# Mask by quadrants, a product on three tiles at once, and a recomputed order in an attention and two-MLP kernel

## The chip, the cores and the metric

One core of a Trainium2 chip runs the whole program. The metric is the device time of one execution in microseconds, a median of several runs. TensorE (PE) multiplies, VectorE (DVE), ScalarE (ACT) and GpSimd (POOL) work on elements, and SyncE (SP) issues every DMA. Each engine has its own list of instructions and works through it in that order.

## The reference

Three layers follow each other, in float32. The matrices of the MLPs come as float64 and are turned into float32 on the chip.

```
scores = q @ k.T / sqrt(64)          # 4 batches, 8 heads, 576 rows, head size 64
keep score (i, j) where 0 <= i - j < 64, else -1e9; softmax; attn @ v
x  = attention as 2304 x 512
h  = x @ w_in                        # first MLP, 512 -> 1024
solu = h * softmax(h); ln = layer norm(solu) * g_ln
x2 = ln @ w_out                      # 1024 -> 512, "the second product of the first MLP"
h  = x2 @ w_in                       # second MLP, 512 -> 2048
g  = (a0 + a1 h + a2 h^2 + a3 h^3) / (1 + |b0||h| + |b1|h^2 + 1e-6)
out = g @ w_out                      # 2048 -> 512
```

## The kernel before

The 2304 rows are 18 tiles of 128. Every product of float32 accuracy is made as three products of halves: the operand is split into a rounded high part and a low rest (`wi`, `xh`/`xl`, `lh`/`ll`), and high x high, low x high and high x low are added up in one PSUM bank.

Two phases follow each other on TensorE.

**Phase one** takes the 18 tiles through attention and the first MLP. A tile t goes through `scores` (tile `s`, lines 295 to 312: the mask is added first, line 304, as a product with an identity matrix of 128 rows, then 16 products of 64 x 64 quarters of the array, line 309), the row maximum on VectorE (`soft_max`), eight exponentials on ScalarE, the sums' reciprocals on VectorE (`soft_sum`, tile `rc`), the scaling on GpSimd (`soft_norm`, line 334), transposes on TensorE (`pt`), copies, `attend` (`pv`), the split (`xh`, `xl`), the first product (`h`, lines 441 to 451, 24 products of 512 columns into one single PSUM tile `h`), the solu and layer norm (`st`, `e`; VectorE and ScalarE in turn), transposes (`pl`), their split (`lh`, `ll`), and for each pair of tiles the second product (`x2_mm`, lines 521 to 530; the trace calls its output `x`). That one has four blocks `dc`, each of 24 products of 256 columns, and its result goes to memory (`x2d`).

The float64 weights are converted by a chain of steps on ScalarE and VectorE for each piece of 128 x 512 (`cv_step`, lines 391 to 418; `cv_hi`, `cv_lo`): eight pieces `wi` of the first MLP's first matrix, eight pieces `wo` of its second one, and 32 pieces `cc` of the second MLP, which are spilled to memory (`w2d`). All eight `wi` are needed for the first `h`, all eight `wo` for the first block of `x2`.

**Phase two** runs the second MLP in six blocks of three tiles (`g_mm` with output `hp`, `o_mm` with output `o`). Its weights are loaded back from `w2d` and split (`w2_hi`, `w2_lo`, tile `w`), its inputs from `x2d` (`x_hi`, `x_lo`, tiles `x2h`, `x2l`).

The order of all this is not written out. Each step is added to a planner (class `Schedule`, lines 31 to 158) with its engines, a duration, the steps it needs, the buffers it takes and gives back (the rings in `RINGS`) and, for some, a wanted time from the tables `WANT` and `PACE`. `latest` works out a due time for each step, `arrange` picks, engine by engine, the step that is due first of those that could start, and the instructions are emitted in that order. A step with two engines, as `"DVE|POOL"`, goes to the second where the planner thinks that it is free sooner.

Of the kernel before, what the change touches and what calls it, by code (L numbers as in the profile page):

```python
# [28 lines left out]
class Schedule:  # L29
# [15 lines left out]
    def add(self, key, engine, dur, want, needs, fn, *args, take=(), give=()):  # L45
        assert key not in self.steps, key
        self.steps[key] = [engine.split("|"), dur if isinstance(dur, tuple) else (dur,), want, list(needs), fn, args,
                           take, give]
        for g in give:
            self.givers.setdefault(g, []).append(key)  # L50

    def latest(self):
# [35 lines left out]
        return due  # L88
# [80 lines left out]
RINGS = {"q": 2, "k": 2, "v": 4, "s": 1, "P": 2, "tr": 2, "PT": 4, "o": 2, "x": 2, "h": 1, "e": 2, "lnT": 3, "xs": 1,  # L169
# [5 lines left out]
def attention_moe_moe2(ctx: ExitStack, tc, q, k, v, w1, w1o, g_ln, w2, w2o, num, den, out):  # L175
# [61 lines left out]
    masks = ap.tile([P, 3, P], BF16, name="masks", tag="masks", bufs=1)  # L237

    def constants():
# [11 lines left out]
        for i in range(3):  # L251
            for b in range(2):
                rows = slice(64 * b, 64 * b + 64)
                nc.gpsimd.tensor_copy(masks[rows, i, :], band[rows, 64 * b:64 * b + P])

        nc.gpsimd.memset(masks[0:64, 1, 0:64], NEG)
        nc.gpsimd.memset(masks[64:128, 2, 0:64], NEG)

    def mask_of(t):
        return masks[:, 1 if t * P % S == 0 else 2 if (t * P + 64) % S == 0 else 0, :]  # L260
# [34 lines left out]
    def scores(t):  # L295
# [7 lines left out]
        for j in range(2):  # L303
            nc.tensor.matmul(s[j], ib, mask_of(t).unsqueeze(1).broadcast_to([P, NPAIR, P]), start=True, stop=False)
# [27 lines left out]
    def soft_norm(t, j, eng):  # L332
        sl = slice(NPAIR * j, NPAIR * j + NPAIR)
        eng.tensor_tensor(out=Pn[t][:, j], in0=Pn[t][:, j],  # L334
                          in1=stat[t][2][:, sl].unsqueeze(2).broadcast_to([P, NPAIR, P]), op=ALU.mult)
# [48 lines left out]
    def w1_load(c):  # L384
# [3 lines left out]
        for hf in range(2):  # L388
            tiles["cv", ("i", c, hf)] = x[:, hf, :]

    def cv_step(key, part, eng=None):
# [28 lines left out]
    def cv_hi(key, scale, eng):  # L420
        hi, lo = hi_lo(key)
        A = tiles["cv", key][4]
        if scale is None:
            copy(eng, hi, A)
        elif eng is nc.scalar:
            eng.activation(hi, A, AF.Copy, scale=scale)
        else:
            eng.tensor_scalar_mul(hi, A, scale)

    def cv_lo(key, scale, eng=None):  # L430
        hi, lo = W[key][:, 0, :], W[key][:, 1, :]
        if scale is None:
            sub(eng, lo, tiles["cv", key][4], hi)
# [98 lines left out]
    def x2_out(pr, dc, eng):  # L532
        if dc == 0:
            tiles["xs", pr] = mp.tile([P, 2, KC, P], F32, name=f"xs{pr}", tag="xs", bufs=1)
        copy(eng, tiles["xs", pr][:, :, dc, :], tiles["x2", pr, dc].rearrange("p (t c) -> p t c", t=2))

    def x2_store(pr):
        nc.sync.dma_start(x2d[:, 2 * pr:2 * pr + 2], tiles["xs", pr])
# [4 lines left out]
    for t in range(NTILE):  # L543
        def step(name, engine, dur, needs, fn, *args, want=None, take=(), give=()):
            needs = [n if isinstance(n, tuple) else (n, t) for n in needs]
            want = None if want is None else H0 + t * T + want
            add((name, t), engine, dur, want, needs, fn, *args, take=take, give=give)

        pr, c0 = divmod(t, 2)
# [8 lines left out]
        step("scores", "PE", 1.45, ["load_q", "load_k", ("constants", 0)], scores, t, want=WANT["scores"],  # L558
             take=[("s", t), ("P", t)], give=[("q", t), ("k", t)])
        for j in range(2):  # L560
            step(f"max{j}", "DVE", 0.8, ["scores"], soft_max, t, j)
            for n in range(4):
                step(f"exp{j}{n}", "ACT", 0.58, [f"max{j}"], soft_exp, t, j, n, give=[("s", t)])
            step(f"sum{j}", "DVE", 0.35, [f"exp{j}{n}" for n in range(4)], soft_sum, t, j)
            step(f"norm{j}", "POOL|DVE", (1.15, 0.6), [f"sum{j}"], soft_norm, t, j)
        for j in range(2):
            step(f"probs{j}", "PE", 0.45, [f"norm{j}"], probs_T, t, j, want=WANT[f"probs{j}"], take=[("tr", (t, j))],
                 give=[("P", t)])
            step(f"probs_copy{j}", "ACT|DVE", (0.58, 0.62), [f"probs{j}"], probs_copy, t, j, take=[("PT", (t, j))],
# [3 lines left out]
        step("att_hi", "ACT|DVE", (0.58, 0.62), ["attend"], attended_hi, t)  # L573
        step("att_lo", "DVE", 0.62, ["att_hi"], attended_lo, t, give=[("o", (t, 0))])
# [4 lines left out]
        step("solu_max", "DVE", 1.2, ["h3"], solu_max, t, take=[("e", t)])  # L579
        step("solu_exp", "ACT", 1.3, ["solu_max"], solu_exp, t)  # L580
# [329 lines left out]
```

## Time and profile before

| | us |
|---|---|
| median of 3 runs | 739.9 (738.57 to 739.94) |
| the profiled execution, own time | 739.92 |
| its span, first to last instruction | 738.1 |
| TensorE busy | 699.2 |
| VectorE busy | 615.2 |
| ScalarE busy | 487.6 |
| GpSimd busy | 64.9 |

The profile lists each instruction with its start, its duration and, where its engine stood idle before it, what ended the wait. Products on TensorE overlap, so that the price of one is the distance from its start to the next start, not its own duration. The span is 1.8 us shorter than the execution's time.

### The profile page before, as it was taken

How to read it: one execution, taken by the hardware profiler on the slowest of the kernel's cores; microseconds unless marked ns; L12 is line 12 of the kernel's file. 1: busy time of each engine (PE TensorE's matmuls, PEld its weight loads, DVE VectorE, ACT ScalarE, POOL GpSimd, SP SyncE). 2: the span in 40 equal slices, each digit the busy share in tenths (PEclk: the TensorE clock that was granted, in tenths of full speed). 3: DMA queues.
4: the chain of work that ended last, by engine and by line, in shares of the span. 5: the costliest groups of instructions: out<-in, count | busy, mean ns of one | idle time of the engine just before them, and what ended most of it. 6: DMA issues, size and time to landing. Idle time of an engine off the chain costs nothing.

```text
span 738.1 us, 12597 instructions
## 1 busy us (share of the span) xinstructions
PE 699.2 (95%) x4788; PEld 620.6 (84%) x4788; DVE 615.2 (83%) x1016; ACT 487.6 (66%) x970; POOL 64.9 (9%) x65
## 2 busy tenths in 40 slices
PE   1578999999999999999999999999999999999997
PEld 0356788888888888999888999989899889998985
DVE  5999999999999665688999878788877797777874
ACT  5587777777777554586888556665676566666553
POOL 2211111111111111001521000000000000000000
PEclk9999999999999999999999999999999999999999
DMA  8554387878776320345420100100010010001001
GB/s 302 198 188 148 115 266 234 292 240 258 263 235 208 116 86 30 115 143 154 140 71 23 65 0 22 64 2 0 22 65 1 0 52 15 0 1 44 1 0 44
DMA packets 47644, 77.90 MB, mean 106 GB/s; under 512 B 5024, under 2 KB 23456, under 8 KB 47072
## 3 DMA queue, kind: packets, MB, share of 16 engines
q1 hardware_dynamic: 47584, 77.09, 32.1%
q8 instruction: 38, 0.62, 0.4%
q14 instruction: 22, 0.18, 0.1%
HBM read 59.25 MB, written 17.83 MB: 104 GB/s over the span
## 4 chain that ended last, share of the span: by engine, by line
PE 85%; DVE 7%; DMA 3%; ACT 2%; issue 1%; SPq 1%; POOL 0%; DVEq 0%; ACTq 0%; POOLq 0%
PE hp L721 8%; PE hp L720 8%; PE hp L719 8%; PE o L785 8%; PE o L784 8%; PE o L783 8%; PE x L527 5%; PE x L529 5%; PE x L528 5%; PE h L449 4%; PE h L451 4%; PE h L450 4%; PE s L309 3%; PE pv L357 2%; PE pl L509 2%; PE pt L340 2%
## 5 line engine op out<-in xcount | busy, mean ns | idle before, releaser
L721 PE MATMUL hp<-x2h,w 128*128 128x384 f32 x384 | 129.6, 337 | 1.2 <-DVE w L210 1.1
L719 PE MATMUL hp<-x2h,w 128*128 128x384 f32 x384 | 129.3, 337 | 0.0
L720 PE MATMUL hp<-x2l,w 128*128 128x384 f32 x384 | 129.2, 337 | 0.0
L729 ACT ACTIVATE w<-hp,ab 128x768 f32<-128x768 f32 x48 | 43.4, 904 | 115.3 <-PE hp L721 115.1
L785 PE MATMUL o<-w,gl 128*128 128x512 f32 x288 | 113.8, 395 | 0.0
L784 PE MATMUL o<-w,gh 128*128 128x512 f32 x288 | 113.5, 394 | 0.0
L783 PE MATMUL o<-w,gh 128*128 128x512 f32 x288 | 113.2, 393 | 0.0
L737 DVE SCALAR_TENSOR_TENSOR w<-r,b,w 128x768 f32<-128x768 f32 x48 | 49.6, 1033 | 54.9 <-ACT r L731 54.9
L527 PE MATMUL x<-lh,wo 128*128 128x256 f32 x288 | 83.9, 291 | 0.0
L529 PE MATMUL x<-lh,wo 128*128 128x256 f32 x288 | 81.3, 282 | 0.0
L528 PE MATMUL x<-ll,wo 128*128 128x256 f32 x288 | 81.0, 281 | 0.0
L719 PEld LDWEIGHTS hp<-x2h,w 128*128 128x128 f32 x384 | 72.1, 188 | 3.3
L720 PEld LDWEIGHTS hp<-x2l,w 128*128 128x128 f32 x384 | 72.1, 188 | 3.3
L721 PEld LDWEIGHTS hp<-x2h,w 128*128 128x128 f32 x384 | 72.1, 188 | 1.9 <-DVE w L210 1.9
L785 PEld LDWEIGHTS o<-w,gl 128*128 128x128 f32 x288 | 54.0, 188 | 12.6
L449 PE MATMUL h<-wi,xh 128*128 128x512 f32 x144 | 59.2, 411 | 5.1 <-DVE st L466 4.4
L784 PEld LDWEIGHTS o<-w,gh 128*128 128x128 f32 x288 | 54.0, 188 | 9.8
L334 POOL TENSOR_TENSOR P<-P,rc 128x512 f32<-128x512 f32 x36 | 40.5, 1125 | 247.3 <-DVE rc L330 195.0
L783 PEld LDWEIGHTS o<-w,gh 128*128 128x128 f32 x288 | 54.1, 188 | 9.4
L451 PE MATMUL h<-wi,xl 128*128 128x512 f32 x144 | 57.9, 402 | 0.7 <-DVE xl L210 0.7
L450 PE MATMUL h<-wi,xh 128*128 128x512 f32 x144 | 57.5, 399 | 0.0
L323 ACT ACTIVATE P<-s,mx 128x128 f32<-128x128 f32 x144 | 50.7, 371 | 9.7 <-DVE mx L318 7.7
(109 smaller groups left out, 1522.3 us busy)
## 6 DMA issues: line engine op xcount, KB each, us to landing
v<-in_v_dram SPq DMA_DIRECT2D x35, 256.0 KB, 4.4
xc<-in_moe_w_in_dram SPq DMA_DIRECT2D x16, 512.0 KB, 4.3
xc<-in_moe_w_out_dram SPq DMA_DIRECT2D x16, 512.0 KB, 4.1
w2d<-Ac SPq DMA_DIRECT2D x32, 256.0 KB, 3.8
r<-w2d SPq DMA_DIRECT2D x32, 256.0 KB, 3.0
k<-in_k_dram SPq DMA_DIRECT2D x17, 384.0 KB, 4.0
q<-in_q_dram SPq DMA_DIRECT2D x18, 256.0 KB, 5.1
x2d<-xs SPq DMA_DIRECT2D x9, 512.0 KB, 3.9
```

What stands on the lines that cost most here:

```text
L449: nc.tensor.matmul(o, xh[:, c, :], wh, start=(c == 0), stop=False)
L450: nc.tensor.matmul(o, xh[:, c, :], wl, start=False, stop=False)
L451: nc.tensor.matmul(o, xl[:, c, :], wh, start=False, stop=(c == KC - 1))
L527: nc.tensor.matmul(o, wh, lh[:, f, :], start=(f == 0), stop=False)
L528: nc.tensor.matmul(o, wh, ll[:, f, :], start=False, stop=False)
L529: nc.tensor.matmul(o, wl, lh[:, f, :], start=False, stop=(f == FC1 - 1))
L719: nc.tensor.matmul(h, wh[:, sl], xh[:, c], start=(c == 0), stop=False)
L720: nc.tensor.matmul(h, wh[:, sl], xl[:, c], start=False, stop=False)
L721: nc.tensor.matmul(h, wl[:, sl], xh[:, c], start=False, stop=(c == KC - 1))
L783: nc.tensor.matmul(o, gh[:, n, sl], wh, start=(f == 0), stop=False)
L784: nc.tensor.matmul(o, gh[:, n, sl], wl, start=False, stop=False)
L785: nc.tensor.matmul(o, gl[:, n, sl], wh, start=False, stop=(f == FC2 - 1))
```

## The change

- The mask is added by four products of 64 x 64 quarters of the array instead of two of the whole one. Each still streams 512 columns; the mask table has two patterns instead of three and is chosen for each half tile.
- The second product of the first MLP takes three tiles at once: four blocks of 24 products of 384 columns for each three tiles. The tiles `lh` and `ll` grow from 256 to 384 columns and have two buffers instead of three.
- GpSimd keeps the scaling `soft_norm` and the constants; the low parts `w2_lo`, `x_lo` and `cv_lo` stay on VectorE. Steps `cv0` and `cv_hi` of the conversions are ScalarE's alone.
- The first matrix is loaded in eight halves of 512 KB instead of four pieces of 1 MB.
- The planner's durations are replaced, and a new table `SHIFT` of some 560 numbers, one for each kind of step (the first five tiles, the last two, and the rest by class), moves its due time.

```
-            nc.tensor.matmul(s[j], ib, mask_of(t).unsqueeze(1).broadcast_to([P, NPAIR, P]), start=True, stop=False)
+            for b in range(2):
+                rows, cols = slice(64 * j, 64 * j + 64), slice(64 * b, 64 * b + 64)
+                nc.tensor.matmul(s[j][cols], ib[rows, rows], mask_of(t, b)[rows].unsqueeze(1).broadcast_to([64, NPAIR, P]),
+                                 start=True, stop=False)
...
-        o = po.tile([P, 2 * P], F32, name=f"x2_{pr}_{dc}", tag="o")
+        o = po.tile([P, TB], F32, name=f"x2_{pr}_{dc}", tag="o")
...
-        if t % 2 == 1:
+        if c0 == JT - 1:
...
-        x = mp.tile([P, 2, 512], I64, name=f"xi_{c}", tag=("lh", "ll")[c % 2], bufs=3)
-        nc.sync.dma_start(x, w1[c * P:(c + 1) * P, :].rearrange("p (h f) -> p h f", h=2))
+            tiles["w1", c] = mp.tile([P, 2, 512], I64, name=f"xi_{c}", tag=("lh", "ll")[c % 2], bufs=2)
+        x = tiles["w1", c][:, hf, :]
+        nc.sync.dma_start(x, w1[c * P:(c + 1) * P, 512 * hf:512 * hf + 512])
...
-        add(("w2", i), "DVE|POOL", (0.602, 1.225), due + 0.7, [("w2h", i)], w2_lo, f, j, give=[("r2", ("w", i))])
+        add(("w2", i), "DVE", 0.68, due + 0.7, [("w2h", i)], w2_lo, f, j, give=[("r2", ("w", i))])
...
-            add(("x", bk, c), "DVE|POOL", (0.45, 0.956), due + 4.0, [("xh", bk, c)], x_lo, bk, c, give=[("xr", (bk, c))])
+            add(("x", bk, c), "DVE", 0.55, due + 4.0, [("xh", bk, c)], x_lo, bk, c, give=[("xr", (bk, c))])
...
-                due[key] = min([cap.get(key, 1e9)] + ([st[2]] if st[2] is not None else []) +
-                               [due[u] - after for u in users[key]])
+                due[key] = min([cap.get(key, 1e9)] + [due[u] - after for u in users[key]] +
+                               ([st[2] + SHIFT.get(st[8], 0.0)] if st[2] is not None else []))
...
-RINGS = {"q": 2, "k": 2, "v": 4, "s": 1, "P": 2, "tr": 2, "PT": 4, "o": 2, "x": 2, "h": 1, "e": 2, "lnT": 3, "xs": 1,
+SHIFT = {
+    "k_zero.0": 29.34, "v_zero.0": 33.59, "load_q.0": 16.46, "load_k.0": 8.1, "load_v0.0": 62.31, "load_v1.0": 28.99,
...
+RINGS = {"q": 2, "k": 2, "v": 4, "s": 1, "P": 2, "tr": 2, "PT": 4, "o": 2, "x": 2, "h": 1, "e": 2, "lnT": 2, "xs": 1,
```

The instruction lists show where things move. In the names, the first number behind a letter is the tile (`h5`), for `x2` the group of tiles and the block; the last number is a serial one.

TensorE at the start of a tile's scores (`s0_0`, `s0_1`: the two banks). Before, of the first scores in its list:

```order
L304 LDWEIGHTS ib_96
L304 MATMUL s1_0_157<-masks_97,ib_96 128x512
L304 LDWEIGHTS ib_96
L304 MATMUL s1_1_158<-masks_97,ib_96 128x512
L309 MATMUL s1_0_157<-k1_128,q1_130 64x128 x2
L309 MATMUL s1_1_158<-k1_128,q1_130 64x128 x2
```

and in the changed kernel:

```order
L409 LDWEIGHTS ib_96
L409 MATMUL s0_0_179<-masks_97,ib_96 64x512
L409 LDWEIGHTS ib_96
L409 MATMUL s0_0_179<-masks_97,ib_96 64x512
L409 LDWEIGHTS ib_96
L409 MATMUL s0_1_180<-masks_97,ib_96 64x512
L409 LDWEIGHTS ib_96
L409 MATMUL s0_1_180<-masks_97,ib_96 64x512
L415 MATMUL s0_0_179<-k0_140,q0_151 64x128 x2
L415 MATMUL s0_1_180<-k0_140,q0_151 64x128 x2
```

Two weight loads and two products of 128 rows have become four of 64 rows, and all stand ahead of the quarter products as before.

TensorE around the first block of the second product (`x2_0_0`). Before:

```order
L449 MATMUL h3_869<-wi_3_1_430,xh3_833 128x512
L450 MATMUL h3_869<-wi_3_1_430,xh3_833 128x512
L451 MATMUL h3_869<-wi_3_1_430,xl3_834 128x512
L509 MATMUL pl2_0_930<-ident_95,e2_819 128x128 x4
L509 MATMUL pl2_1_939<-ident_95,e2_819 128x128 x4
L527 MATMUL x2_0_0_947<-lh0_648,wo_0_489 128x256
L528 MATMUL x2_0_0_947<-ll0_649,wo_0_489 128x256
L529 MATMUL x2_0_0_947<-lh0_648,wo_0_489 128x256
```

and in the changed kernel:

```order
L415 MATMUL s8_1_1302<-k8_1082,q8_1047 64x128 x2
L415 MATMUL s8_0_1301<-k8_1082,q8_1047 64x128 x2
L415 MATMUL s8_1_1302<-k8_1082,q8_1047 64x128 x2
L415 MATMUL s8_0_1301<-k8_1082,q8_1047 64x128 x2
L415 MATMUL s8_1_1302<-k8_1082,q8_1047 64x128 x2
L629 MATMUL x2_0_0_1338<-lh0_790,wo_0_642 128x384
L630 MATMUL x2_0_0_1338<-ll0_791,wo_0_642 128x384
L631 MATMUL x2_0_0_1338<-lh0_790,wo_0_642 128x384
```

Before, the block stands behind the first product of tile 3 (`h3`) and the transposes of tile 2. In the changed kernel it stands behind `h5` and the scores of tile 8: ahead of it stand scores of 9 tiles, 15 half transposes `pt`, 7 `pv`, 6 `h` and 3 tiles' `pl`, where there were 5, 8, 4, 4 and 3.

VectorE at the last piece `wo`, which that block needs. Before:

```order
L494 TENSOR_SCALAR st2_818<-st2_818 128x1
L435 SCALAR_TENSOR_TENSOR wo_5_880<-Ao_5_766,gT_98,wo_5_880 128x512
L499 TENSOR_SCALAR e2_819<-e2_819,st2_818 128x1024
L435 SCALAR_TENSOR_TENSOR wo_6_892<-Ao_6_779,gT_98,wo_6_892 128x512
L435 SCALAR_TENSOR_TENSOR wo_7_899<-Ao_7_808,gT_98,wo_7_899 128x512
L317 TENSOR_REDUCE mx4_702<-s4_0_705 128x4
L318 TENSOR_SCALAR mx4_702<-mx4_702 128x4
L457 TENSOR_REDUCE st3_944<-h3_869 128x1
```

and in the changed kernel:

```order
L522 ISA Ao_5_820<-co_5_819,ro_5_821 128x1024
L522 ISA Ao_6_1125<-co_6_1124,ro_6_1126 128x1024
L522 ISA Ao_2_1111<-co_2_1110,ro_2_1112 128x1024
L537 SCALAR_TENSOR_TENSOR wo_5_1282<-Ao_5_820,gT_98,wo_5_1282 128x512
L537 SCALAR_TENSOR_TENSOR wo_6_1287<-Ao_6_1125,gT_98,wo_6_1287 128x512
L537 SCALAR_TENSOR_TENSOR wo_2_1295<-Ao_2_1111,gT_98,wo_2_1295 128x512
L423 TENSOR_REDUCE mx8_1298<-s8_0_1301 128x4
L424 TENSOR_SCALAR mx8_1298<-mx8_1298 128x4
```

The last `wo` was row 159 of VectorE's list and is row 203.

SP's queue at the last loads `xo`, from which the last `wo` are made. Before:

```order
L381 DMA xo_4_574<-in_moe_w_out_dram 128x512
L279 DMA k5_581<-in_k_dram 128x4x192
L271 DMA q5_587<-in_q_dram 128x512
L381 DMA xo_5_617<-in_moe_w_out_dram 128x512
L381 DMA xo_6_631<-in_moe_w_out_dram 128x512
L381 DMA xo_7_664<-in_moe_w_out_dram 128x512
L293 DMA v4_0_689<-in_v_dram 128x512
L293 DMA v4_1_727<-in_v_dram 128x512
```

and in the changed kernel:

```order
L396 DMA v4_1_640<-in_v_dram 128x512
L382 DMA k4_720<-in_k_dram 128x4x192
L396 DMA v5_0_769<-in_v_dram 128x512
L396 DMA v5_1_797<-in_v_dram 128x512
L374 DMA q6_877<-in_q_dram 128x512
L374 DMA q7_886<-in_q_dram 128x512
L487 DMA xo_2_933<-in_moe_w_out_dram 128x512
L487 DMA xo_6_967<-in_moe_w_out_dram 128x512
L396 DMA v6_0_1007<-in_v_dram 128x512
```

The last `xo` stood behind `q5` and ahead of the values of tile 4; the last two now stand behind the keys of tile 4, the values of tile 5 and the queries of tiles 6 and 7.

## Rows read from the trace of the kernel before

**Rows 1.** Stretches: length, each engine's busy time (instructions), granted clock, DMA share, GB/s.
```profile
0.00:84.70 84.70, 52.06 (x451) 38.66 (x451) 73.81 (x162) 57.65 (x150) 14.08 (x28) 0.96 0.60 207
84.70:240.00 155.30, 155.28 (x1538) 137.57 (x1536) 150.24 (x359) 115.20 (x329) 22.75 (x20) 1.00 0.73 237
...
320.00:400.00 80.00, 78.77 (x444) 72.93 (x443) 74.89 (x86) 62.37 (x92) 19.75 (x9) 1.00 0.36 104
```
**Rows 2.** Timeline of TensorE at its first second product: start, duration, instruction.
```profile
84.68 0.36 PE L527 MATMUL x<-lh,wo 128*128 128x256 f32 x1
```
**Rows 3.** The chain of waits, one step (`pt`) of two neighbouring tiles: start, duration.
```profile
122.53 0.87 PE pt L340 x8
...
138.36 0.87 PE pt L340 x8
```
**Rows 4.** Timeline of TensorE within one tile of the steady part.
```profile
153.35 0.39 PE L449 MATMUL h<-wi,xh 128*128 128x512 f32 x1
...
154.04 1.03 PE L340 MATMUL pt<-ident,P 128*128 128x128 f32 x8
154.83 0.36 PE L527 MATMUL x<-lh,wo 128*128 128x256 f32 x1
...
157.78 0.61 PE L304 MATMUL s<-masks,ib 128*128 128x512 bf16 x2
158.32 1.10 PE L309 MATMUL s<-k,q 64*64 64x128 f32 x32
159.35 1.15 PE L357 MATMUL pv<-PT,v 128*64 128x64 f32 x32
160.44 0.39 PE L527 MATMUL x<-lh,wo 128*128 128x256 f32 x1
```
**Rows 5.** Timeline of TensorE in phase two: twelve products of 384 columns, then the next.
```profile
481.33 0.33 PE L719 MATMUL hp<-x2h,w 128*128 128x384 f32 x1
...
483.44 0.39 PE L783 MATMUL o<-w,gh 128*128 128x512 f32 x1
```
**Rows 6.** Timeline of VectorE: its first instruction, and the last two pieces `wo`.
```profile
7.42 0.43 DVE L411 TENSOR_SCALAR ci<-ci 128x512 f32<-128x512 f32 x1 [7.42 <-ACT ci L404]
...
82.01 1.41 DVE L435 SCALAR_TENSOR_TENSOR wo<-Ao,gT,wo 128x512 fp32r<-128x512 f32 x2
```
**Rows 7.** VectorE's groups: busy time, mean ns of one | idle before.
```profile
L457 DVE TENSOR_REDUCE st<-h 128x1 f32<-128x1024 f32 x18 | 22.0, 1220 | 11.3 <-PE h L451 11.3
L466 DVE CUSTOM_DVE_ANT_0 e<-h,e 128x1024 f32<-128x1024 f32 x18 | 21.9, 1219 | 5.7 <-ACT e L461 5.7
```
**Rows 8.** Timeline of VectorE: a row maximum up to the next instruction; reciprocals likewise.
```profile
12.13 0.68 DVE L317 TENSOR_REDUCE mx<-s 128x4 f32<-128x512 f32 x1
...
12.93 0.69 DVE L210 TENSOR_TENSOR wi<-Ai,wi 128x512 fp32r<-128x512 f32 x1
...
61.50 0.16 DVE L329 TENSOR_SCALAR rc<-sum 128x4 f32<-128x4 f32 x1
...
61.81 1.22 DVE L466 CUSTOM_DVE_ANT_0 e<-h,e 128x1024 f32<-128x1024 f32 x1
```
**Rows 9.** VectorE's groups that the change takes away ahead of the last `wo`.
```profile
L406 DVE TENSOR_SCALAR co<-xo 128x512 uint32<-128x512 uint32 x2 | 1.7, 835 | 0.0
L216 DVE CAST wi<-Ai 128x512 fp32r<-128x512 f32 x1 | 1.3, 1264 | 0.0
L406 DVE TENSOR_SCALAR ci<-xi 128x512 uint32<-128x512 uint32 x1 | 1.3, 1260 | 0.0
```
**Rows 10.** Timeline of GpSimd and VectorE: a low part on GpSimd, and two equal instructions on VectorE.
```profile
348.12 3.35 POOL L210 TENSOR_TENSOR x2l<-xr,x2h 128x384 fp32r<-128x384 f32 x1 [54.39 <-ACT x2h L702]
...
350.50 1.78 DVE L762 SCALAR_TENSOR_TENSOR t<-t,ab,r 128x768 f32<-128x768 f32 x1
...
370.99 1.01 DVE L762 SCALAR_TENSOR_TENSOR t<-t,ab,r 128x768 f32<-128x768 f32 x1
```
**Rows 11.** DMA issues of the `xo` loads: count, KB each, median us to landing.
```profile
xc<-in_moe_w_out_dram SPq DMA_DIRECT2D x16, 512.0 KB, 4.1
```

More of the change, by code (lines that the diff above doesn't have):

```diff
@@ L87, in latest @@
                         cap[g] = min(cap.get(g, 1e9), d - steps[g][1][0] - self.LATENCY)
-        return due
+        return {k: d + (SHIFT.get(steps[k][8], 0.0) if steps[k][2] is None else 0.0) for k, d in due.items()}
     def arrange(self):
@@ L250, in constants, with mask_of @@
         )
[L251 to L260, printed above, removed]
+        for i in range(2):
+            for j in range(2):
+                rows = slice(64 * j, 64 * j + 64)
+                nc.gpsimd.tensor_copy(masks[rows, i, :], band[rows, 64 * j:64 * j + P])
+        nc.gpsimd.memset(masks[:, 1, 0:64], NEG)
+    def mask_of(t, b):
+        return masks[:, 1 if (t * P + 64 * b) % S == 0 else 0, :]
     raw, values, Pn, stat, PTs, xTs, tiles = {}, {}, {}, {}, {}, {}, {}
@@ L545, in step @@
             needs = [n if isinstance(n, tuple) else (n, t) for n in needs]
-            want = None if want is None else H0 + t * T + want
-            add((name, t), engine, dur, want, needs, fn, *args, take=take, give=give)
-        pr, c0 = divmod(t, 2)
+            if want is not None:
+                want += H0 + t * T
+            cls = str(t) if t < 5 or t > LAST - 2 else f"s{t % JT}" if want is not None else "s"
+            add((name, t), engine, dur, want, needs, fn, *args, take=take, give=give, group=f"{name}.{cls}")
+        pr, c0 = divmod(t, JT)
         if t == 0:
@@ L609, in convert @@
     def convert(key, want, load, last):
+        group = "cv." + "_".join(map(str, key))
         if load is not None:
-            add(("cvl", *key), "DMA", 1.46, None, [], cv_load, key, load, take=[("x64", key)])
-        cvl = ("cvl", *key) if load is not None else ("cvl", *key[:-1])
+            add(("cvl", *key), "DMA", 1.46, None, [], cv_load, key, load, take=[("x64", key)], group=group)
+        cvl = ("cvl", *key)
         give = [("x64", key)] if load is not None else []
-        for part, engine, dur, needs in [(0, "ACT|DVE", (0.67, 0.6), [cvl]), ("r", "ACT", 0.67, ["cv0"]), (1, "DVE", 0.34, ["cv0"]),
-                                         (2, "DVE", 0.34, ["cv1"]), (3, "DVE", 0.62, ["cv2"]), (6, "DVE", 0.62, ["cv3", "cvr"])]:
+        for part, engine, dur, needs in [(0, "ACT", 0.61, [cvl]), ("r", "ACT", 0.61, ["cv0"]), (1, "DVE", 0.42, ["cv0"]),
+                                         (2, "DVE", 0.42, ["cv1"]), (3, "DVE", 0.69, ["cv2"]), (6, "DVE", 0.68, ["cv3", "cvr"])]:
@@ L616, in convert @@
             needs = [(n, *key) if isinstance(n, str) else n for n in needs]
             add((f"cv{part}", *key), engine, dur, None, needs, cv_step, key, part,
[L618 removed]
+                take=[("cA", key)] if part == 0 else [], give=give if part in ("r", 3) else [], group=group)
         needs = [("cv6", *key)]
         if last is cv_spill:
[L621 removed]
+            add(("cv7", *key), "DMA", 0.73, want, needs, cv_spill, key, key[1], give=[("cA", key)], group=group)
@@ L840, in step @@
             needs = [n if isinstance(n, tuple) else (n, p) for n in needs]
-            add((name, p), engine, dur, due, needs, fn, bk, f // 2, *args, take=take, give=give)
+            add((name, p), engine, dur, due, needs, fn, bk, f // 2, *args, take=take, give=give,
+                group=f"{name}.{p if p < 5 else 's'}")
         step("g_pre0", "ACT", 0.82, s0 + 2.0, [("g", i)], g_pre, 0, take=[(r, p) for r in ("gw", "gr", "gt")])
@@ L858, in attention_moe_moe2 @@
             add(("o", i2), "PE", 2.08, s3 + (U / 2 if i2 == i else 0.0), needs, o_mm, bk, f,
-                take=[] if f else [("o2", (bk, j)) for j in range(JT)], give=[("gh", p)])
+                take=[] if f else [("o2", (bk, j)) for j in range(JT)], give=[("gh", p)],
+                group=f"o.{i2 if i2 < 10 else 's'}")
         if f == FC2 - 1:
```

127 lines of the change are left out of this document (62 added, 65 removed), and 95 rows, old and new, of the table SHIFT.

## The prediction

> **What bounds the kernel now.** I read the busy times by stretches first [rows 1]: from 84.7 us to 320 TensorE is never idle, and from there to the end it loses 1.2 us up to 400 and its last wait is the output's copy and store. Only the first 84.7 us are loose: TensorE is busy for 52.1 of them, with a mean granted clock of 0.96, while VectorE is busy for 73.8. The stretch ends where TensorE begins its first second product, at 84.68 [rows 2], right after VectorE has made the last piece `wo` (82.01 + 1.41 = 83.4) [rows 6]. So there are two regimes: a start paced by VectorE, which converts weights, and then 650 us in which time is TensorE's work and nothing else. In the steady part a tile takes 138.36 - 122.53 = 15.83 us [rows 3].
>
> With that, time is: start of the first second product (X), plus TensorE's work that is left at X, plus the tail. Before: X = 84.7, and 738.1 - 84.7 = 653.4 us behind it.
>
> **The mask.** Two products of the whole array take 158.32 - 157.78 = 0.54 us [rows 4]. Four quarter products of 512 columns aren't in the trace. The floor is one product of 512 columns, 0.23 us (three `h` products in 154.04 - 153.35 = 0.69), the ceiling four one behind the other, 0.92 [rows 4]. In between: quarter products of the scores start every (159.35 - 158.32) / 32 = 0.032 us, whole ones of the same 128 columns (`pt`) every (154.83 - 154.04) / 8 = 0.099 [rows 4], so quarters overlap 3.1-fold, and four mask products should take 0.92 / 3.1 = 0.30. I take that, since the scores alternate over the same four quarters: 0.24 us less a tile, from 0.31 less to 0.38 more.
>
> **Second product on three tiles.** One block of 24 products of 256 columns takes 157.78 - 154.83 = 2.95 us [rows 4]; four of them serve two tiles, 5.90 a tile. Twelve products of 384 columns take 483.44 - 481.33 = 2.11 in phase two [rows 5], 24 take 4.22, and four blocks serve three tiles: 5.63. That is 0.27 a tile, 18 x 0.27 = 4.9 us in all; the row has the same shape and the same operand types, so I leave 0.1 a tile as its uncertainty. Both together bring the tile from 15.83 to 15.32.
>
> **The start, X.** The changed order puts more attention ahead of the first second product. VectorE's list up to the last `wo` grows from 159 rows to 203. Added: 8 row maxima with their scaling, 12.93 - 12.13 = 0.80 each [rows 8], 6.4; 7 reciprocal pairs, 61.81 - 61.50 = 0.31 [rows 8], 2.2; 3 `xl` and 2 `ll` of 0.69 (as the `wi` subtraction of the same shape) [rows 8], 3.5; 2 maxima over `h` and 2 `solu_mul` of 1.22 [rows 7], 4.9; and some 10 small `st` instructions, 2 us (an estimate from the reciprocals). That is 19.0. Gone: two `co` of 0.84, one `ci` of 1.26, one `wi` cast of 1.26 [rows 9] and one `PT` copy of the `wi` subtraction's 0.69 [rows 8], 4.9, which pass to ScalarE, busy for 57.7 of 84.7 us [rows 1]. Net 14.1. GpSimd's scaling runs seven times more in that stretch, and a VectorE instruction beside GpSimd's work is held: 1.78 against 1.01 us for the same instruction [rows 10]; 0 to 0.77 each, 0 to 5.4 in all, I take 2. The first load is half as large, so VectorE's start at 7.42 [rows 6] should come earlier; before, it waited for the whole 1 MB, and I take 1.5 off. VectorE was idle for 84.7 - 73.8 - 7.4 = 3.5 us more [rows 1, 6], which a fuller list may use or not. X moves by 14.1 + 2 - 1.5 = 14.6, to 99 (92 to 106).
>
> That later X isn't a loss, since TensorE has done more by then: 4 scores of 159.35 - 157.78 = 1.57, 7 half `pt` of 0.40, 3 `pv` of 160.44 - 159.35 = 1.09 and 2 `h` of 24 x 0.23 = 5.5 [rows 4], 6.3 + 2.8 + 3.3 + 11.0 = 23.4 us that were behind X. The start thus wins 23.4 - 14.6 = 8.8 (between 2 and 16).
>
> **GpSimd off the splitting.** Nine low parts, 19.75 us of GpSimd [rows 1], go to VectorE: four `w` of 0.69 [rows 8] and five `x2l`, 384 columns instead of 512, at three quarters of that: 5.3 us in the stretch 320 to 400, where VectorE has 80 - 74.9 = 5.1 idle [rows 1]. But each GpSimd one holds a VectorE instruction by about 0.77 (1.78 against 1.01) [rows 10], nine times 6.9 at most, so VectorE's sum hardly changes. TensorE's loss there was 1.2 [rows 1]; I leave it, with 0 to 4.
>
> **Edits at nothing.** The halved loads cost four more issues on SP, early; the `lh`/`ll` rings hold six tiles as before; the 14 `xs` and 10 conversion steps that leave VectorE land on ScalarE, busy for 115.2 of 155.3 us [rows 1]. If ScalarE were full, each would hold a PSUM buffer and with it TensorE.
>
> **The sum.** Behind X: 653.4 - 23.4 (done earlier) - 9 x 0.24 (masks of tiles 9 to 17) - 4.9 = 622.9. The masks of tiles 0 to 8 lie where TensorE waits anyway and give nothing. 99 + 622.9 = 721.9, and 1 us for new short waits (the list now has places where `h` stands 2.2 us behind its `pv`, worked out from the durations above, where it was 3.0): a span of 723. The execution was 1.8 us longer than its span, 739.92 against 738.1, and equals the median, so 725. With X from 92 to 106 this is 718 to 732.
>
> **Rivals.**
>
> *The start gives nothing.* If TensorE can't use the cover, because `h` has one PSUM tile that `solu_mul` on VectorE gives back (a maximum, an exponential and a multiply after each `h`, two of them 1.22 [rows 7]), then X moves on by all the 23.4 us, to 108. Five `h` in a row must pass through that before X. Only the product and the masks behind X pay: 738.1 - 4.9 - 2.2 = 731.0, time 733. For it: VectorE is full there. Against: the attention of the tiles ahead doesn't need that buffer, and VectorE's own sum says 99.
>
> *VectorE becomes the bound behind X.* From 84.7 to 240 it is busy for 150.2 of 155.3 us [rows 1], so a faster TensorE may only find it late. Then 155.3 / 15.83 = 10 tiles lose their 0.51: 5 us, time 730. The Trainium skill's page "TensorEngine Tiling (Array Packing)" has a rule for this, in "PSUM Bottleneck" under "Performance Considerations": packing speeds TensorE up but not the emptying of PSUM, which may become the limit. By that rule the time is this 730; no run here shows it yet. Against: 14 `xs` copies and other work leave VectorE, about 10 us by the price of such copies (0.4 to 0.7 each), so that its load falls below 95%.
>
> *The mask quarters don't overlap.* 0.92 a tile: the 9 masks behind X cost 3.4 instead of giving 2.2, time 731.
>
> *The loads come late, and it is slower.* The last two `xo` now stand in SP's queue behind the queries of tiles 6 and 7, and a query load needs the buffer that the scores of two tiles before give back. Tile 4's scores must then run before the queries of tile 6, and those ahead of both `xo`. A load lands in 4.1 us [rows 11], then ScalarE and VectorE need some 4 us for a piece. The first VectorE step of these pieces is row 172 of 203; the 32 rows from there, at the prices above, are some 14 us, so they are wanted from about 84 on, and the scores of tile 4 may run up to about 78. Each us after that moves X one for one, since all of `x2` waits for the last `wo`. The old time is reached at X = 115, that is with these scores at about 95; I price it at X = 118, 744.
>
> **How the numbers follow.** The forecast has 0.56, the start without gain 0.14, VectorE as the bound 0.11, the mask 0.06, late loads 0.08; 0.05 is left for what I don't see, about as often the same as faster. About 0.2%, 1.5 us, is what a measurement of this kernel can tell from no change. Faster is 0.56 + 0.14 + 0.11 + 0.06 + 0.02 = 0.89, less 0.02 for a tail of those that reaches no change: 0.87; same 0.05; slower 0.08. The range goes from 714 (X at 92, masks at the floor, the loss at 320 to 400 gone, and a little less held time on VectorE) to 735, which takes in the three rivals on the faster side and leaves out the slow one.
>
> **What would show it.** In the profile of the changed kernel: the first `x2` product near 99 us, right behind the last `wo`; a mask's four products in 0.30; a `x2` block in 4.22; TensorE without waits from there on, and a phase two as long as before. X beyond 107, TensorE waiting for VectorE between 100 and 300 us, a mask above 0.5, or a wait for `xo` at 80 to 100 would each make the prediction wrong in its own term.

## The result and the profile after

| | before | after |
|---|---|---|
| median, us | 739.36 (738.57 to 739.94) | 731.58 (731.00 to 732.53) |
| ratio to before, 95% interval | | 0.9897 (0.9880 to 0.9914) |
| the profiled execution, its span | 738.1 | 730.7 |
| X, the start of the first second product | 84.68 | 106.95 |
| the span behind X | 653.4 | 623.75 |
| VectorE busy up to X, and idle | 73.8, 10.9 | 90.2, 16.7 |

The changed kernel is faster by 1%. The forecast was 725 with a range of 714 to 735. What it missed stands in one line of the table: X is 106.95 and not 99, just outside the 92 to 106 that the prediction gave it. The span behind X came out as forecast in its sum.

The stretches of the changed kernel answer to [rows 1], in the same columns (length, busy time of PE, PEld, DVE, ACT and POOL with instructions, granted clock, DMA share, GB/s):

```profile
0.00:84.70 84.70, 53.41 (x536) 41.84 (x536) 69.16 (x155) 60.20 (x178) 17.74 (x29) 0.96 0.60 191
84.70:240.00 155.30, 152.53 (x1385) 134.70 (x1382) 144.45 (x326) 115.70 (x327) 21.42 (x18) 1.00 0.66 214
320.00:400.00 80.00, 80.00 (x410) 73.37 (x410) 69.21 (x87) 58.13 (x85) 0.00 (x0) 1.00 0.29 88
```

VectorE is less busy in the first 84.7 us than before (69.2 against 73.8), although it has more to do ahead of X. TensorE's loss between 320 and 400 is gone. In the second stretch TensorE misses 2.8 us, 1.5 of it still ahead of X and 1.3 in one wait behind it, for VectorE's `e`.

TensorE around X and further on, to be read against [rows 2, 4]: its last wait ahead of X, the last masks ahead of X, the first second product, a whole block of it (from 119.49 to the next work at 123.83, with the first of each three products at 120.12 and 120.65), the masks of a later tile with the scores behind them, and the starts of two blocks that follow each other:

```profile
98.55 1.15 PE L463 MATMUL pv<-PT,v 128*64 128x64 f32 x30 [0.86 <-ACT PT L317]
...
105.74 0.41 PE L409 MATMUL s<-masks,ib 64*64 64x512 bf16 x4
...
106.95 0.44 PE L629 MATMUL x<-lh,wo 128*128 128x384 f32 x1
...
119.49 0.44 PE L629 MATMUL x<-lh,wo 128*128 128x384 f32 x1
...
120.12 0.34 PE L629 MATMUL x<-lh,wo 128*128 128x384 f32 x1
...
120.65 0.34 PE L629 MATMUL x<-lh,wo 128*128 128x384 f32 x1
...
123.83 0.60 PE L611 MATMUL pl<-ident,e 128*128 128x128 f32 x4
...
155.67 0.41 PE L409 MATMUL s<-masks,ib 64*64 64x512 bf16 x4
155.91 1.04 PE L415 MATMUL s<-k,q 64*64 64x128 f32 x32
...
315.60 0.34 PE L629 MATMUL x<-lh,wo 128*128 128x384 f32 x1
...
319.83 0.34 PE L629 MATMUL x<-lh,wo 128*128 128x384 f32 x1
```

VectorE's last three `wo` pieces, which answer to [rows 6]:

```profile
105.23 2.07 DVE L537 SCALAR_TENSOR_TENSOR wo<-Ao,gT,wo 128x512 fp32r<-128x512 f32 x3
```

They end at 107.30, 0.35 us behind X, and TensorE doesn't wait for them: it works without a break from 98.55 until well behind X. Before, the last `wo` ended at 83.42 and TensorE worked without a break up to X too, from its last wait, for VectorE's solu, at 76.61:

```profile
76.61 0.70 PE L449 MATMUL h<-wi,xh 128*128 128x512 f32 x1 [1.70 <-DVE st L466]
```

So in neither kernel is X the moment at which TensorE is released by the last `wo`. X is where TensorE's own list comes to the second product, after all its waits for VectorE, ScalarE, GpSimd and loads.

What VectorE waited for up to X (in total, times, longest), first in the kernel before, then in the changed one:

```profile
DVE ci L411 <- ACT ci L404: 7.4, 1, 7.4
DVE st L457 <- PE h L451: 1.0, 1, 1.0
DVE mx L317 <- PE s L309: 0.5, 1, 0.5
DVE wi L210 <- ACT wi L214: 0.4, 1, 0.4
DVE wo L435 <- ACT wo L426: 0.2, 1, 0.2
```

```profile
DVE ci L515 <- ACT ci L510: 7.5, 2, 5.5
DVE wi L313 <- ACT wi L528: 3.8, 2, 3.6
DVE mx L423 <- PE s L415: 1.0, 3, 0.5
DVE ll L313 <- ACT lh L317: 1.0, 1, 1.0
DVE st L559 <- PE h L553: 0.6, 1, 0.6
```

The first line has two parts, 5.47 for the first half piece of the first matrix and 2.05 for the second one:

```profile
9.97 0.43 DVE L515 TENSOR_SCALAR ci<-ci 128x512 f32<-128x512 f32 x1 [2.05 <-ACT ci L510]
```

One wait is new and long: 3.6 us of a `wi` subtraction for ScalarE. The timeline of ScalarE, VectorE and TensorE at that place, one line each, shows what ScalarE was doing:

```profile
35.98 0.20 ACT L794 ACTIVATE b<-ab 128x1 f32<-128x1 f32 x1 [3.82 <-DMA ab<-in_moe_b_dram]
```

```profile
39.55 0.69 DVE L313 TENSOR_TENSOR wi<-Ai,wi 128x512 fp32r<-128x512 f32 x1 [3.59 <-ACT wi L528]
```

```profile
39.57 0.50 PE L551 MATMUL h<-wi,xh 128*128 128x512 f32 x1 [3.22 <-ACT wi L528]
```

ScalarE stood for 3.82 us at one instruction of 128 numbers, the absolute value of a coefficient of the second MLP (`b1`), which VectorE first reads at 313.5 us. Its operand was still in flight. The chain of waits has that load as a piece of 8 us:

```profile
27.99 7.97 DMA ab<-in_moe_b_dram
```

Before, the same instruction waited 1.1 us. The planner can't see it: the step `coefficients` is entered as a DMA step, and the ScalarE instruction is written inside it, right behind the load. ScalarE comes to that instruction whether the load has landed or not, and waits there. Behind it stood `co`, `PT`, exponentials and the `wi` cast for which VectorE and then TensorE waited.

### The profile page after: what moved, and what is told of

It is laid out like the page before. It is cut to its first block, busy times and chain, and to the rows that moved or that the text cites. A ratio compares the mean times of both kernels' runs of the same rounds, so it can differ in the third digit from the quotient of the medians.

```text
span 730.7 us, 12007 instructions
## 1 busy us (share of the span) xinstructions
PE 691.6 (95%) x4536; PEld 617.9 (85%) x4536; DVE 613.1 (84%) x997; ACT 496.8 (68%) x986; POOL 46.6 (6%) x53
## 4 chain that ended last, share of the span: by engine, by line
PE 88%; ACT 4%; DMA 3%; DVE 3%; SPq 1%; issue 1%; POOL 1%; POOLq 0%; ACTq 0%; DVEq 0%
PE hp L825 9%; PE hp L824 9%; PE hp L823 9%; PE o L889 9%; PE o L888 9%; PE o L887 9%; PE x L629 4%; PE x L631 4%; PE x L630 4%; PE h L551 4%; PE h L552 4%; PE h L553 4%; PE pl L611 2%; PE pv L463 2%; PE s L415 2%; PE pt L446 2%
## 5 line engine op out<-in xcount | busy, mean ns | idle before, releaser
L629 PE MATMUL x<-lh,wo 128*128 128x384 f32 x192 | 66.9, 349 | 0.0
L631 PE MATMUL x<-lh,wo 128*128 128x384 f32 x192 | 65.0, 339 | 0.0
L630 PE MATMUL x<-ll,wo 128*128 128x384 f32 x192 | 65.0, 338 | 0.0
L888 PEld LDWEIGHTS o<-w,gh 128*128 128x128 f32 x288 | 54.0, 188 | 10.9
L440 POOL TENSOR_TENSOR P<-P,rc 128x512 f32<-128x512 f32 x36 | 42.7, 1185 | 221.8 <-DVE rc L436 151.3
```

The source lines that it names most:

```text
L629: nc.tensor.matmul(o, wh, lh[:, f, :], start=(f == 0), stop=False)
L630: nc.tensor.matmul(o, wh, ll[:, f, :], start=False, stop=False)
L631: nc.tensor.matmul(o, wl, lh[:, f, :], start=False, stop=(f == FC1 - 1))
L888: nc.tensor.matmul(o, gh[:, n, sl], wl, start=False, stop=False)
```

## The experiments

Kernels of one group shared a chip and the runs of the kernel before, whose median was 739.5 to 739.7 in all three groups. The changed kernel has only the runs of the table, on another chip with 739.36 for the kernel before, so differences to it of some 0.3 us say nothing. Numbers in brackets are lowest and highest.

### First group: what made X late

**coef_late** takes the ScalarE instruction, and a small VectorE one beside it, out of the step with the loads; they are emitted behind the last product `h` of tile 8:

```
+        order.insert([k for k, _ in order].index(("h3", 8)) + 1, ("coefficients_abs", "ACT"))
...
         nc.sync.dma_start(ab[:, 0:4], num.partition_broadcast(P))
         nc.sync.dma_start(ab[:, 4:6], den.partition_broadcast(P))
+
+    def coefficients_abs():
         nc.scalar.activation(b1, ab[:, 5:6], AF.Abs)
         nc.vector.memset(qe, QEPS)
```

> The changed kernel in its own order, but ScalarE's one small instruction on the second MLP's coefficients (tile b) and the memset beside it are emitted behind the first product of tile 8; their two loads stay where they are in SP's queue. In the trace of the changed kernel ScalarE waits 3.8 us for that load at 32 to 36 us, with the conversions and copies of the start queued behind. Theory 1, the start is late because of two transfers (this one, and the first query tile): the first second product moves from 107 to about 103.5 and the time from 731.6 to about 728. Rival, VectorE's list and the single PSUM tile of h set that moment anyway: other waits take its place, time 731 to 732.

Measured: 728.46 us (728.07 to 729.11), ratio 0.9852 (0.9839 to 0.9865), X = 103.61. The 3.8 us wait is gone from VectorE's list, and X and the median both fell by about 3.1 to 3.3. In its place stand short waits that the later VectorE uncovers:

```profile
DVE ci L526 <- ACT ci L521: 7.1, 2, 5.6
DVE st L570 <- PE h L564: 1.7, 1, 1.7
DVE mx L434 <- PE s L426: 1.2, 3, 0.6
DVE wo L548 <- ACT wo L541: 0.5, 1, 0.5
DVE wi L324 <- ACT wi L539: 0.4, 2, 0.2
```

Theory 1 holds: this wait is one cause, with its size, some 3.2 of the 8 us by which X was missed.

**q_first** lets the first query and key load ahead of all but one of the half pieces of the first matrix (in the changed kernel they stand behind four of them, and the first scores begin at 13.56):

```
+        move(("k_zero", 0), None)
+        move(("load_k", 0), ("cvl", "i", 0, 0))
+        move(("load_q", 0), ("cvl", "i", 0, 0))
```

> The changed kernel in its own order, but the first query and key tiles are loaded right behind the first half piece of the first matrix, ahead of three more half pieces. Theory 1: the first scores start near 9.5 us instead of 13.6; the conversion of the second half piece comes about 1.7 us later (512 KB at 300 GB/s); the first second product moves 2 to 3 us ahead, time 728.5 to 730. Rival: weights and not scores pace the start, time 731 to 734.

Measured: 730.11 us (729.34 to 731.99), X = 105.65. The scores ran 6.2 us earlier and X came 1.3 earlier. The time lies between theory 1 and its rival, and its interval of 0.9863 to 0.9891 overlaps that of the changed kernel, so the medians alone don't show a gain. TensorE's next wait took the rest (timeline of TensorE):

```profile
7.35 1.98 PE L425 MATMUL s<-k,q 64*64 64x128 f32 x32 [2.17 <-DMA k<-in_k_dram]
19.61 1.12 PE L456 MATMUL pt<-ident,P 128*128 128x128 f32 x4 [10.27 <-POOL P L450]
```

The 10.27 is put down to GpSimd's scaling, but that is only the last link: the row maximum ran at 14.47 on VectorE, behind conversion steps, and the exponentials behind it.

**coef_q** is both edits.

> Both edits. Theory 1: the two gains add up, the first second product at about 100 to 102, time 724.5 to 727. Rival: no gain, 731 to 733.

Measured: 727.84 us (727.04 to 730.02), ratio 0.9840 (0.9827 to 0.9852), the lowest median of all. By medians the two edits gave 3.1 and 1.5 alone, and 3.7 together, less than theory 1 wanted. It isn't clear of coef_late, whose interval it overlaps; its profiled execution was the longest of its five (730.02), with X at 105.13 against coef_late's 103.61. That q_first adds anything to coef_late isn't shown.

**mask_whole** is the changed kernel with the old mask, two products of the whole array.

> The changed kernel in its own order with the mask added by two products of the whole array again: 0.54 us a tile instead of 0.24. If only work behind the first second product counts: the nine masks of tiles 9 to 17 cost 2.7 us, time 734.3, and that product still starts near 107. If the masks of the first nine tiles count too: 5.4 us, 737.

Measured: 734.59 us (732.45 to 736.57), X = 107.92: 3.0 us more than the changed kernel. Nine masks behind X at 0.54 - 0.24 = 0.30 are 2.7, so the first expectation is near and the second, 737, is not. In the profiled executions TensorE is busy behind X for 619.70 us against 617.42, 2.3 more, and X is 1.0 later, so that a part of the 3.0 lies in the start.

### Second group: the first chain, the order, and two parts alone

**early_chain** is coef_q with tile 0's maxima, exponentials, sums, scaling and copies moved ahead of conversion steps:

```
+        chain(("cv6", "i", 0, 0), *t0("scores", "max1", "max0"))
+        chain(("cv6.5", "i", 0, 0), *t0("exp11", "exp10", "exp13", "exp12", "exp03", "exp00", "exp02", "exp01"))
+        chain(("cv3", "i", 2, 0), *t0("sum1", "norm1", "probs1"))
+        chain(("cv1", "i", 0, 1), *t0("sum0", "norm0", "probs0"))
+        chain(("cvr", "i", 1, 0), *t0("probs_copy1", "probs_copy0"))
```

> The changed kernel with the two repairs of coef_q (coefficients' Abs emitted late, first query and key loaded right behind the first half piece), and in addition tile 0's maxima, exponentials, sums, scaling and copies moved ahead of the conversion steps on VectorE and ScalarE. In q_first and coef_q the first scores ran at 7.35 us but the first transposes only at 19.6, since the maxima stood behind conversion steps (14.5). Theory 1 (every us by which the first tile's chain is earlier is a us of the start): first transposes at 13 to 15, X at 99 to 102, 723 to 726. Rival (TensorE has nothing else to do then, since the second tile's chain and the eight wi pieces keep their times on a full VectorE): X 103 to 105, 727 to 728.5.

Measured: 728.75 us (727.09 to 729.85), the same as coef_q and coef_late, with X = 102.65. The first transposes did run at 14.40 instead of 19.6, and TensorE then waited at the next places (timeline of TensorE):

```profile
14.40 1.11 PE L470 MATMUL pt<-ident,P 128*128 128x128 f32 x4 [5.28 <-POOL P L464]
...
23.06 0.69 PE L487 MATMUL pv<-PT,v 128*64 128x64 f32 x16 [1.87 <-DMA v<-in_v_dram]
28.17 0.63 PE L433 MATMUL s<-masks,ib 64*64 64x512 bf16 x2 [4.43 <-ACT P L453]
```

Theory 1 falls by its time: 5 us won at the first transposes didn't shorten the kernel. VectorE's work ahead of X stays at some 89.5 to 90.2 us in all these kernels.

**no_shift** is the changed kernel with the table emptied (`SHIFT = {}`), so that the planner orders by its durations and by the wanted times in `WANT` and `PACE`, which are those of the kernel before.

> The changed kernel with the table of shifts empty, so that the order follows from the new durations alone. Its list has 177 VectorE rows up to the last wo piece instead of 204, and on TensorE three scores, five half transposes, one attend and one h less, and two pl more, ahead of the first second product: some 11 us of TensorE's work. Theory 1 (in the start VectorE's work sets X, and TensorE's work moved ahead of X is paid for about one to one): X about 96, the rest longer by 11, 731 to 733, apart from waits behind X. Rival (the table is worth what the prediction gave the start): 737 to 741.

Measured: 755.41 us (751.37 to 757.39), ratio 1.0209 (1.0183 to 1.0236). Both expectations are wrong. X was 93.20, 13.8 us earlier than in the changed kernel. Behind it TensorE is busy for 639.01 us against 617.42, of which some 3.4 are for a lower clock (0.83, 0.88 and 0.95 in three slices of 10 us), so that 18.2 us of its work had moved behind X and the start lost 4.5. The rest went behind X: TensorE is idle there for 17.4 us against 6.4, and with the 3.4 for the clock the account is 4.5 + 11.0 + 3.4 = 18.9, all of what the profiled execution is longer by. That execution took 751.37, the shortest of the five; why the others took up to 6 us more wasn't followed. The longest waits (behind 93 us; in the changed kernel there is one, of 1.3 us, in the same part):

```profile
PE h L450 <- DVE st L467: 3.2, 2, 1.9
PE h L450 <- ACT P L328: 2.6, 1, 2.6
PE h L450 <- DVE st L479: 1.4, 1, 1.4
```

**x2_three** is the kernel before with the second product on three tiles. With it go the buffers that it needs, as in the changed kernel: `lh` and `ll` of 384 columns in two buffers instead of three, and two instead of three for the pieces of the first matrix that share their place; and the planner orders all steps anew, with the new durations of this product and its copies.

```
-        o = po.tile([P, 2 * P], F32, name=f"x2_{pr}_{dc}", tag="o")
+        o = po.tile([P, TB], F32, name=f"x2_{pr}_{dc}", tag="o")
...
-        if t % 2 == 1:
+        if c0 == JT - 1:
...
-                step(f"x2_{dc}", "PE", 2.86, needs + [("cv7", "o", c) for c in range(FC1)], x2_mm, pr, dc,
+                step(f"x2_{dc}", "PE", 4.2, needs + [("cv7", "o", c) for c in range(FC1)], x2_mm, pr, dc,
```

> The kernel before with only the second product on three tiles at once (lh and ll of 384 columns in two buffers, the first matrix's pieces in the same two). Theory: blocks of 24 products of 384 columns instead of 256 give back 5.90 - 5.6 = 0.3 a tile on TensorE, all 18 tiles behind X, 5 us: 734.7, with X later only by work that TensorE has done by then. Rival (three tiles must be ready instead of two before the first block, with as much idle TensorE ahead of X as the extra tile takes): 737 to 740.

Measured: 762.86 us (762.55 to 763.72), ratio 1.0317 (1.0303 to 1.0331): 23 us slower, far beyond both expectations. X was 92.69. Behind it TensorE loses 13.6 us up to 320 and 3.1 up to 400, half of it at the transposes `pl`, for which VectorE makes `e` (waits from 92 us to 400):

```profile
PE pl L509 <- DVE e L499: 8.4, 5, 3.2
PE h L449 <- DVE st L466: 3.7, 2, 2.6
PE hp L721 <- DVE w L210: 2.1, 4, 1.0
```

The waits cost more than their own length: each of the three stretches of lower clock behind X stands right behind one of the longest waits. Three slices of this kernel, ten us each:

```profile
110.00:120.00 10.00, 10.00 (x80) 8.61 (x79) 9.53 (x21) 7.12 (x24) 1.49 (x2) 1.00 0.86 291
120.00:130.00 10.00, 6.64 (x90) 5.74 (x90) 9.79 (x25) 8.25 (x28) 1.15 (x1) 0.91 0.63 205
130.00:140.00 10.00, 10.00 (x43) 8.46 (x42) 8.00 (x16) 3.44 (x8) 2.35 (x2) 0.75 0.84 309
```

In the second slice TensorE is busy for 6.64 of 10 us, and in the third it is busy all the time at a mean of 0.75, between its levels of 1.2 and 2.4 GHz. Over all slices with a lower clock behind X (0.91, 0.75, 0.83, 0.87, 0.96 of 10 us each) that is some 6.8 us of work. The account goes by what lies behind X. TensorE is busy there for 646.53 us against 647.18 before; without the 6.8 for the clock, and with 3.3 won by the product itself (see below), it had done 4.2 us more of its work by X, which is 8.0 later, so the start lost 3.8. With 15.9 more of idle time behind X (22.2 against 6.3), 6.8 for the clock and 3.3 won that is 23.2 of the 23.3 by which the span is longer. Which part of the edit makes the waits, the wider product, the buffers or the order that the planner makes of them, isn't shown.

**quarter_mask** is the kernel before with the mask by quarters, and nothing else.

> The kernel before with only the mask by quarters, in its old order. The masks took 0.54 us a tile and take 0.24. Theory (only what lies behind X counts): 5 of the 18 tiles have their scores ahead of X there, 13 x 0.30 = 3.9: 735.8. Rival (those ahead of X count too): 18 x 0.30 = 5.4: 734.3. A second rival (VectorE, busy for 150 of 155 us behind X there, is found late): 738 to 739.

Measured: 735.14 us (734.56 to 735.74), ratio 0.9940 (0.9927 to 0.9952): 4.5 us less, between the first expectation (3.9) and its rival (5.4). The trace splits it: the span behind X is 649.6 against 653.4, 3.9 less for the thirteen masks there, and X is 0.9 earlier, at 83.80 (one execution of each). The second rival is out: from X to 240 VectorE is busy for 98%, and TensorE hardly waits.

```profile
83.80:240.00 156.20, 156.14 (x1584) 140.55 (x1583) 152.97 (x369) 117.10 (x341) 22.75 (x20) 1.00 0.71 242
```

### Third group: GpSimd, and VectorE's list

**split_back** gives the nine low parts that GpSimd made before back to it, in the changed kernel:

```
+WPOOL, XPOOL = (23, 24, 28, 31), ((1, 0), (1, 2), (1, 3), (2, 1), (2, 2))
...
-        sub(nc.vector, lo, tiles["r2", f, j], hi)
+        sub(nc.gpsimd if 2 * f + j in WPOOL else nc.vector, lo, tiles["r2", f, j], hi)
...
-        sub(nc.vector, xl[:, c], tiles["xr", bk, c], xh[:, c])
+        sub(nc.gpsimd if (bk, c) in XPOOL else nc.vector, xl[:, c], tiles["xr", bk, c], xh[:, c])
```

> The changed kernel, in its own order, with the nine low parts (five x2l, four w) that GpSimd made in the kernel before given back to GpSimd. Theory 1 (they cost TensorE what it lost there before): TensorE loses about 1.2 us between 340 and 400, 732.8. Rival (VectorE has slack now and TensorE isn't reached): within 0.3 of the changed kernel, 731.6.

Measured: 731.14 us (730.28 to 732.22), ratio 0.9886 (0.9871 to 0.9901), the same as the changed kernel. The stretch from 340 to 400, here and then in the changed kernel:

```profile
340.00:400.00 60.00, 59.60 (x299) 53.66 (x298) 57.73 (x65) 47.42 (x68) 14.30 (x8) 1.00 0.27 82
```

```profile
340.00:400.00 60.00, 60.00 (x302) 54.20 (x301) 57.85 (x73) 48.09 (x69) 0.00 (x0) 1.00 0.29 83
```

VectorE does eight instructions fewer (the ninth lies behind 400) and is busy just as long. Others take longer in their place, as in this group of seven equal instructions, here and then in the changed kernel:

```profile
L868 DVE SCALAR_TENSOR_TENSOR t<-t,ab,r 128x768 f32<-128x768 f32 x7 | 8.3, 1189 | 0.0
```

```profile
L866 DVE SCALAR_TENSOR_TENSOR t<-t,ab,r 128x768 f32<-128x768 f32 x7 | 7.1, 1010 | 0.0
```

What GpSimd takes over, it costs VectorE again in held instructions. TensorE loses 0.4 us in this stretch, for VectorE's `gl`, where it lost nothing in the changed kernel; the time doesn't show it.

**ll_twice** computes six low parts a second time on VectorE:

```
-        sub(nc.vector, tiles["ln", pr][1][sl], tiles["pl", t, hf], tiles["ln", pr][0][sl])
+        for _ in range(2 if t < 3 else 1):
+            sub(nc.vector, tiles["ln", pr][1][sl], tiles["pl", t, hf], tiles["ln", pr][0][sl])
```

> The changed kernel with the six low parts ll of tiles 0 to 2 computed twice on VectorE, the second time over the same place: 6 x 0.60 = 3.6 us more on VectorE ahead of X, which nothing but the first second product waits for. Theory 1 (VectorE's own list sets X, and its 16.7 us of idle time there are waits that can't be filled): X 106.95 + 3.6 = 110.5, 735.2. Rival (another engine's chain sets X, and VectorE's idle time takes the work in): X 107 to 108, 731.6 to 732.6.

Measured: 734.26 us (732.28 to 736.59), 2.7 more than the changed kernel; in the profiled execution X = 109.27, 2.3 later, with VectorE busy for 3.7 us more and idle for 1.4 less. It lies nearer to theory 1: of the 3.7 us added to VectorE ahead of X, 2.3 come out in X, and 1.4 go into its waits. As the six runs spread over 4.3 us, that share is rough.

## Why the prediction was right, and which term failed

The time of 731.58 lies inside the range, but the gain is half of the forecast one (8 us instead of 15), and the range had been drawn to 735 to take in the rivals. X lies outside its own range, and 0.05 us short of the 107 beyond which the prediction calls itself wrong. One of its signs did come: TensorE waits for VectorE for 1.3 us between 100 and 300 us. The forecast had put 1 us there for short waits.

**The model held.** Time is X plus what is left at X. Behind X, 623.9 was forecast (622.9, and 1 for new short waits) and 623.75 measured. In all seven kernels that have the new mask and the new order (X from 102.65 to 109.27) the span behind X stays between 622.7 and 623.8: coef_late 726.3 - 103.61 = 622.7, early_chain 725.3 - 102.65 = 622.7, ll_twice 732.1 - 109.27 = 622.8.

**The term that failed is the start.** It was to win 8.8 us and won about nothing: X moved by 22.3 and TensorE had been busy for 74.17 - 52.04 = 22.1 us more by then (forecast 23.4, at the old price of the masks). The sum for X had two parts, VectorE's work and its idle time. The work was priced right: 73.8 + 14.1 + 2 = 89.9 forecast, 90.2 measured. The idle time was not: 10.9 before, 9.1 in the forecast, 16.7 measured. The 7.6 us between are nearly the whole miss. That sum is an account: VectorE's work and idle time up to X add up to X whoever sets it, and the prediction's reason for going by VectorE, that X follows the last `wo`, isn't what the traces show (see above). That VectorE's list paces the start is shown in part by ll_twice, where 2.3 of 3.7 us come out in X. The parts of the idle time can be read:

- "I take 1.5 off" for the halved first load. VectorE did start at 5.47 instead of 7.42, but then waited 2.05 for the second half piece, 7.5 in all against 7.4. The step took the first instruction's time for the start of the stream. No run undoes the halved load.
- 3.4 more for `wi`, by ScalarE's wait for the coefficients. The prediction had looked at every DMA queue and at GpSimd, and not at a ScalarE instruction that moves with a DMA step. coef_late shows it: 3.1 us.
- The rest, some 2.6, are short waits for ScalarE and TensorE (`mx`, `ll` and others, at most 1.0 each) and gaps. "VectorE was idle for 3.5 us more, which a fuller list may use or not" was the place to ask for a bound. ll_twice shows that a fuller list uses little of it: of 3.7 us more work the idle time took 1.4 in. The cause of these 2.6 stays open.

**The rival "the start gives nothing"** had the right outcome (X = 108, 733) by a wrong mechanism. It wanted TensorE waiting for `solu_mul` to give `h` back; that wait is 1.5 us in the changed kernel, and was 4.4 before. **Late `xo` loads** cost nothing: no engine waits for them up to X.

**The mask**: 0.30 forecast, 0.24 measured (four products from 155.67 to 155.91 in the steady part), so four quarters of 512 columns take what one product of 512 columns takes in `h`, 0.23 [rows 4]. They overlap fully, where the forecast took the 3.1-fold of the scores with 0.23 as its floor.

**The product on three tiles** was mis-sized. The forecast took 24 products as twice the twelve of [rows 5], 4.22; a block takes 4.34 in the steady part, since the first product of a block is slower there (120.12 - 119.49 = 0.63 for the first three products, 0.53 for each three that follow). The block of 315.60, which stands behind products of the second MLP, has no such first product and takes 319.83 - 315.60 = 4.23, the forecast's price. The blocks of phase one stand behind attention work (`pt`, `pl`, `pv`, scores), as those of 256 columns did; the forecast's 2.95 had that first product in it [rows 4], its 4.22 hadn't. The 36 blocks of before sum to 107.2 us, the 24 of after to 103.9 without one wait in them: 3.3 won instead of 4.9. Two other things made up for it: the masks gave more, and TensorE's 1.2 us at 320 to 400 went. That the sum behind X came out to 0.2 us is in this part luck.

**GpSimd off the splitting**: nothing, as forecast, and for the reason given ("VectorE's sum hardly changes"): split_back. The 1.2 us that TensorE lost before in that stretch go mostly with the old order: with GpSimd back in the new order it loses 0.4.

**VectorE as the bound behind X** didn't come. It is busy for 144.45 of 155.3 us from 84.7 to 240, and even at 98% in quarter_mask TensorE didn't wait. The Trainium skill's page "TensorEngine Tiling (Array Packing)" warns in "PSUM Bottleneck" under "Performance Considerations" that packed products may be limited by the emptying of PSUM; the traces of these two kernels don't show that behind X. In x2_three, though, VectorE is busy for 134.15 of 140 us from 100 to 240, 96%, and TensorE does wait for it: up to 400, 8.4 us at `pl` and 3.7 for the one PSUM tile of `h`. A full VectorE alone doesn't say whether TensorE waits.

**What the prediction didn't ask** is what the order is worth. It took TensorE without waits behind X as a fact of the kernel, and it is one of this order: the same steps without the table take 755, and the old kernel with the wider product 763. The gain of the three-tile product wasn't to be had alone, in the order that the old planner makes. Why the planner places `e` and `st` late in these two kernels wasn't followed further.

**A better version.** coef_late and coef_q beat both kernels: 728.46 and 727.84 us, against 731.58 and 739.4. The first is a move of two instructions and worth 3 us; what the second adds lies within the spread.

## What to carry to other kernels

When a change fills the list of the engine that paces a stretch, price its idle time as carefully as its work: list the waits of that stretch, and say for each one whether the new order removes it, moves it or lets something else wait there. When a planner moves a DMA step, look for instructions on other engines that are emitted inside it; they stop their engine wherever the load lands. And a wider product can cost more in waits than it saves: here, without the new order, it was 3 us won on TensorE and a kernel 23 us slower.

## What the runs showed of the hardware

- Four quarter products of 64 rows and 512 columns, spread over the four quarters of the array, take 0.24 us together; one product of 512 columns in `h` takes 0.23.
- A load of 1 KB took 7.97 us from issue to landing. The 384 KB of a key tile, issued 1 us ahead of it, took 8.6, and three 512 KB pieces a little earlier on the same queue 5.4 in the median; the group of [rows 11], with 4.1, is that of the second MLP's pieces `xc` (the `xo` pieces have the same median).
- In x2_three TensorE stood for 3.4 of the 10 us from 120 on, and the granted clock of the next slice was 0.75, though TensorE was busy all through it.
- The clock column can't be read in the start. Up to some 33 us the products of the changed kernel take about twice their later time, 1.92 us for a tile's scores where they take 1.04 at 155.91, though the column says 1.00:

```profile
31.32 1.92 PE L415 MATMUL s<-k,q 64*64 64x128 f32 x32
```

```profile
20.00:40.00 20.00, 12.70 (x130) 9.59 (x130) 15.92 (x34) 14.04 (x44) 4.23 (x4) 1.00 0.79 257
```

Before, it is the same: 1.97 us at 33.89 against 1.10 [rows 4]. So the 0.96 of the start, here and in [rows 1], is too high in both kernels, and TensorE's busy time there counts for less work than its figure. Nor does the column's 0.83 from 20 to 60 us in coef_q, against 0.96 in the changed kernel, show a slower start: coef_q's scores take 1.92 at 21.11 and at 30.20 too.
